# RWKV attention with a gated convolution network: half-row transposes in three sets, receptances and keys by 64-step parts

## The chip, the cores and the metric

The kernel runs on one core of a Trainium2 chip. The metric is the device time of one execution in microseconds (us). A profiled execution gives the trace from which all rows here are taken; its engines are called PE (TensorE, the matrix engine, with PEld for its weight loads), DVE (VectorE), ACT (ScalarE), POOL (GpSimd) and SP (SyncE, which issues nearly all transfers).

## The reference

Inputs are r, k, v, w of shape (4, 8, 768, 48) (batch, heads, steps, head size), u of shape (8, 48), and the weights of a network after it: w_in (384 x 1024), conv_w (3 x 1024), w_out (1024 x 384). The result is (4, 768, 384).

```python
for t in range(S):
    cur = einsum('bhd,bhe->bhde', u[None] * k_t, v_t)
    y[:, :, t] = einsum('bhd,bhde->bhe', r_t, state + cur)
    state = w_t[:, :, :, None] * state + einsum('bhd,bhe->bhde', k_t, v_t)
x = y.transpose(0, 2, 1, 3).reshape(B, S, H * D)
h = maximum(x @ w_in, 0.0)
conv_out = sum over j of conv_w[j] * (h shifted by j - 1 steps, zeros at the ends)
return (h * sigmoid(conv_out)) @ w_out
```

## The kernel before, in words

The 4 x 768 steps are 24 chunks of 128 steps, six to a batch. For each chunk w, k and r are loaded with steps on partitions (tiles `nat`), and TensorE turns them, so that channels lie on partitions and steps along the row: three thirds of 128 channels for each, in a bank of PSUM (`stage_t`, `st["turned"]`: banks wp for decays, kp for keys, rp for receptances). VectorE makes two scans of the decays from wp (L646 backwards, L654 forwards) into the two planes of the tile kr, and multiplies the keys onto plane 0 (L651) and the receptances onto plane 1 (L658). 16-row copies by DMA (L675, "spread") bring the last channels of each head into a fourth third. `stage_b` makes the scores of a chunk on TensorE (L756 for chunks below 8, L764, by halves, from 8 on), puts them under a mask into pm (L796), brings the state forward (L813 or `half_state`, L878), for which the keys are turned back to steps on partitions (bank tb, `turned_back`), and makes the output y of the chunk (L848), which ScalarE and VectorE write as two parts into x (L856, L857).

The network works on eight blocks of 384 steps (`block`). Each of 8 columns of w_in takes three groups of three products (L896), then a chain between ScalarE and VectorE (L908 to L918, `gating`), whose last reader of the bank is the gate L915; three output tiles of a block take eight groups of three products each (L925). A block begins when the x of its chunks and of its neighbours is there, so the first block needs chunks 0 to 3. The weights are brought into two parts of a narrower form first (`convert`, L489 to L497 and L477, L478).

For chunk 8 and later ones (MERGED) the transposes are cut into halves of 64 rows, and two halves that go to different banks run side by side in the two halves of the array. `stage_b` of chunk n issues them for chunk n + 1, together with the way back of chunk n's keys, as two operations of 12 (`f1`, `f2`, function `one_half`). Between the two, VectorE sets the zero columns of wp to zero (`pad`, L598): it waits for `f1`, and `f2` waits for it.

Which operation comes when is not left to a scheduler. `op` only collects operations with what they read and write; `Plan.issue` then issues them in the order of the list ORDER, a number for each operation, and takes the buffer for each new tile from the list PLACES. Every engine works through its own operations in that order. A negative number is a filler product on TensorE (L445), which computes nothing that is used.

Of the kernel before, what the change touches and what calls it, by code (L numbers as in the profile page):

```python
# [25 lines left out]
MERGED = 8  # L26
HALVED = 8
ORDER = [
    1, 3, 2, 49, 174, 173, 5, 7, 6, 8, -8, 11, 19, 14, 180, 53, 10, 13, 50, 15, 18, 20, 16, 51, 9, 177, 0, -8, -8,
    -8, -8, -8, 181, -1, -1, -1, -1, 27, 52, 183, 54, 185, 188, 175, 28, 23, 24, 193, 194, 195, 219, 25, 178, 21,  # L30
    184, 212, 216, 179, 189, 190, 186, 213, 214, 217, 17, 22, 26, 223, -1, -1, -1, -1, 220, -1, -1, -1, 165, 222,
    224, 258, 251, 4, 218, 12, 182, 255, 55, 196, 232, 233, 191, 259, 166, 225, 167, 227, 236, 261, 234, 192, 29,
    221, 203, 168, 170, 228, 169, 58, 204, 205, 253, 252, 200, 235, 197, 201, 171, 187, 71, 198, 65, 257, 229, -2,
    -2, -2, -2, -2, -2, -2, -2, -2, 230, 263, 60, 72, 172, 66, 61, 73, 67, 199, 256, 231, 202, 238, 176, 215, 262,
    56, 59, 237, 57, 267, 242, 206, 208, 209, 245, 264, 266, 268, 269, 207, 271, 272, 74, 68, 239, 69, 244, 243,
    415, 246, 273, 75, 76, 70, 62, 274, 30, 408, 241, 210, 240, 270, 37, 265, 226, 412, 260, 247, 281, 409, 416,
    211, 38, 44, 458, 39, 45, 32, 418, 283, 420, 282, 33, 413, 43, 275, 277, 63, 278, 40, 451, 46, 64, 254, 410,
    453, 452, 77, 419, 248, 421, 423, 279, 280, 286, 287, 276, 455, 31, 249, 414, 41, 288, 284, 250, 436, 424, 289,
    425, 607, 426, 431, 96, 459, 34, 432, 433, 475, 476, 417, 457, 35, 47, 438, 456, 422, -8, -8, 334, 335, 336,
    462, 323, 467, 324, 325, 36, 337, 338, 437, 48, 42, 461, 434, 463, 285, 466, 464, 339, 468, 477, 340, 326, 327,  # L40
    345, 346, 347, 348, 341, 84, 78, 349, 312, 290, 291, 292, 85, 91, 86, 328, 79, 329, 342, 350, 80, 351, 435, 87,
    478, 301, 313, 314, 302, 303, 92, 81, 90, 330, 460, 293, 294, 352, 93, 82, 611, 88, 94, 428, 430, 429, 427, 439,
    83, 89, 95, 109, 315, 441, 110, 614, 295, 331, 111, 296, 411, 445, 446, 442, 472, 474, 469, 470, 473, 471, 454,
    115, 297, 343, 344, 479, 304, 440, 305, 367, 615, 353, 616, 332, 354, 112, 355, 333, 104, 298, 443, 105, 306,
    444, 368, 447, 482, 369, 448, 98, 483, 484, 617, 307, 99, 481, 480, 465, 113, 103, 97, 316, 299, 449, 450, 485,
    486, 487, 308, 488, 356, 357, 358, 522, 523, 500, 489, 490, 524, 501, 502, 106, 114, 100, 609, 300, 107, 613,
    370, 619, 309, 310, 123, 317, 124, 318, 622, 676, 101, 371, 108, 122, 125, 311, 102, 319, 359, 116, 608, 646,
    372, 320, 373, 623, 511, 512, 491, 117, 624, 118, 653, 612, 126, 360, 650, 128, 321, 374, 492, 503, 493, 361,
    375, 362, 618, 620, 513, 654, 656, 631, 119, 120, 363, 364, 376, 655, 648, 647, 134, 674, 675, 365, 514, 135,
    621, 533, 534, 398, 535, 399, 127, 322, 121, 400, 401, 402, 610, 721, 628, 625, 649, 150, 629, 626, 129, 658,  # L50
    130, 661, 136, 494, 137, 142, 366, 131, 377, 536, 651, 525, 515, 141, 526, 132, 495, 496, 138, 652, 139, 133,
    143, 504, 726, 680, 516, 527, 517, 518, 497, 505, 519, 144, 140, 145, 681, 146, 670, 671, 388, 389, 390, 391,
    392, 555, 556, 557, 393, 657, 403, 662, 394, 404, 405, 537, 679, 558, 559, 520, 521, 632, 506, 659, 507, 528,
    635, 637, 529, 538, 663, 539, 508, 560, 530, 561, 395, 636, 540, 541, 406, 396, 566, 567, 568, 685, 641, 686,
    688, 672, 633, 700, 642, 701, 704, 702, 705, 562, 498, 563, 722, 630, 720, 668, 667, 627, 712, 713, 634, 690,
    569, 689, 725, 727, 531, 570, 699, 714, 571, 378, 379, 380, 381, 382, 383, 638, 732, 384, 733, 735, 639, 572,
    749, 640, 750, 753, 751, 754, 385, 544, 545, 546, 669, 769, 665, 771, 664, 666, 678, 710, 770, 532, 761, 673,
    499, 682, 573, 736, 386, 660, 542, 683, 774, 737, 509, 547, 762, 543, 510, 775, 703, 684, 564, 776, 748, 707,
    708, 677, 937, 706, 711, 935, 709, 687, 691, 692, 693, 643, 695, 696, 942, 548, 644, 694, 574, 780, 763, 549,
    697, 550, 698, 781, 551, 940, 645, 552, 587, 588, 589, 783, 740, 577, 760, 757, 758, 759, 724, 756, 755, 723,  # L60
    715, 927, 718, 928, 729, 716, 719, 764, 717, 728, 915, 916, 741, 919, 744, 920, 917, 936, 730, 785, 553, 784,
    742, 914, 743, 731, 941, 777, 766, 779, 565, 767, 768, 765, 578, 579, 580, 734, 782, 788, 581, 590, 591, 738,
    789, 739, 792, 787, 786, 554, 983, 918, 790, 791, 778, 752, 988, 575, 576, 946, 947, 745, 985, 924, 746, 990,
    793, 949, 794, 923, 984, 922, 925, 950, 951, 926, 772, 407, 387, 921, 773, 1191, 975, 592, 593, 594, 747, 795,
    963, 964, 965, 967, 595, 989, 962, 851, 852, 994, 995, 853, 997, 998, 854, 855, 840, 841, 999, 929, 968, 1140,
    1141, 930, 934, 931, 932, 976, 943, 933, 1128, 1129, 1130, 1132, 856, 1133, 857, 796, 842, 843, 844, 845, 797,
    1127, 846, 858, 1146, 1151, 582, 583, 798, 799, 800, 584, 585, 847, 972, 1148, 973, 1147, 1153, 954, 948, 1152,
    1138, 596, 970, 969, 971, 1192, 1193, 939, 974, 1139, 938, 586, 859, 955, 952, 801, 953, 848, 802, 958, 1142,
    807, 808, 809, 818, 860, 810, 957, 811, 819, 820, 1154, 812, 1155, 803, 849, 977, 813, 804, 862, 1157, 1171,
    1172, 1173, 863, 864, 829, 830, 831, 873, 874, 875, 1175, 1158, 821, 956, 944, 865, 822, 814, 1197, 823, 1159,  # L70
    1170, 866, 945, 1176, 815, 850, 1183, 996, 1002, 959, 1240, 1241, 1239, 1179, 1136, 1137, 1134, 987, 1178, 986,
    1135, 1184, 978, 1185, 824, 980, 981, 991, 1231, 979, 861, 1003, 867, 982, 1143, 1145, 1144, 832, 1174, 876,
    833, 1004, 877, 1246, 960, 1245, 1198, 816, 1000, 868, 834, 993, 869, 825, 1005, 992, 1001, 878, 835, 826, 870,
    879, 597, 598, 599, 600, 601, 602, 603, 604, 1006, 1196, 836, 605, 966, 880, 1007, 837, 961, 881, 1202, 1203,
    1008, 1162, 1205, 1163, 1166, 1219, 1156, 1161, 1220, 1223, 1221, 1042, 1064, 1065, 1043, 1044, 1066, 1206,
    1131, 1164, 1207, 1244, 882, 827, 838, 883, 1232, 1279, 1280, 1180, 1177, 1181, 1288, 397, 606, 1454, 1218,
    1165, 1045, 1067, 805, 806, 1046, 1068, 1250, 1160, 1167, 1168, 871, 1224, 1251, 151, 1253, 1267, 1169, 1268,
    1269, 1047, 1271, 1254, 1255, 1075, 1076, 1077, 1020, 1031, 1053, 1054, 1032, 1055, 1021, 1078, 1079, 1266,
    1069, 1048, 1272, 1233, 1080, 1081, 817, 872, 839, 828, 1234, 1186, 1230, 1149, 1182, 1289, 1228, 1187, 1199,
    1188, 1445, 1189, 1190, 1195, 1225, 1287, 1276, 1150, 1229, 1227, 1275, 1194, 1226, 1273, 1503, 1277, 1274, 894,  # L80
    1022, 1009, 1010, 1033, 1011, 1049, 1056, 1057, 1023, 1293, 1270, 1024, 1070, 1071, 1012, 1034, 1035, 1013,
    1201, 1200, 1294, 1281, 1058, 1050, 1082, 895, 896, 1025, 1026, 1059, 1036, 1072, 1014, 1037, 1060, 1083, 1061,
    1015, 1027, 1038, 1016, 1459, 1039, 152, 1028, 1017, 884, 885, 897, 898, 899, 900, 901, 902, 886, 887, 1204,
    1208, 1210, 1258, 1211, 1214, 1212, 1292, 1213, 1247, 1236, 1235, 1209, 888, 889, 1298, 1299, 1259, 1262, 1215,
    1301, 1433, 1249, 1040, 1302, 1248, 1303, 1432, 1260, 1029, 1278, 1453, 1458, 1455, 1501, 1243, 1242, 1238,
    1295, 1237, 1282, 1285, 1284, 1283, 1446, 1286, 1030, 1062, 1493, 1494, 1063, 1252, 890, 891, 904, 905, 906,
    907, 908, 909, 1434, 1435, 1256, 1437, 1438, 1447, 1257, 1300, 1051, 1261, 1216, 1217, 892, 1460, 1084, 1464,
# [234 lines left out]
def rwkv_conv_moe_kernel(  # L322
# [268 lines left out]
    def thirds(t):  # L591
        return t[:, 0:KT * L].rearrange("p (m t) -> p m t", t=L)
# [124 lines left out]
    def stage_b(n):  # L717
# [50 lines left out]
        if MERGED <= after < N:  # L768
# [4 lines left out]
            if "back" in st:  # L773
                reads, wrote = reads + [kr], wrote + [st["back"][3]]
# [16 lines left out]
        if wrote:  # L791
            op("PE", "f2", lambda: one_half(True), [*reads, (nx["turned"][0], 1)], wrote)
            if "back" in st:
                turned_back(n)
# [234 lines left out]
```

## Time and profile before

| What | Value |
|---|---|
| median of 3 runs | 322.68 us (322.6 to 323.31) |
| profiled execution, its own time | 320.73 us |
| span of its trace | 318.6 us |
| PE busy | 310.0 us, 97% of the span |
| DVE busy | 260.9 us, 82% |
| ACT busy | 231.2 us, 73% |
| POOL busy | 207.3 us, 65% |
| first product of the network | 36.28 us after the start |

The span is the time from the first to the last instruction in the trace; the execution's own time is 2.1 us more. Busy times of PE overlap from one matmul to the next, so a duration on PE is no distance; starts are.

### The profile page before, as it was taken

Reading aid. Unit: us, or ns where it says so; the run is one execution under the profiler, and the core shown is the slowest. Engines: PE = TensorE matmul, PEld = TensorE weight load, DVE = VectorE, ACT = ScalarE, POOL = GpSimd, SP = SyncE. Lnnn points to the kernel's source line nnn. Section 1 sums busy time; section 2 is a strip of 40 time slices with the busy share of each in tenths; the row PEclk is TensorE's granted clock in tenths of the full one; section 3 lists DMA queues with packets and bytes.
Section 4 is the critical chain, followed back from the end, with each engine's and each line's share of the span. In section 5 each row is a group of like instructions: output and inputs, shape, how many; then the busy total and the mean of one; then the engine's idle time right before and its main releaser. Section 6 shows DMA issues by size and latency. Waiting matters only on the chain.

```text
span 318.6 us, 11367 instructions
## 1 busy us (share of the span) xinstructions
PE 310.0 (97%) x4470; PEld 288.6 (91%) x4470; DVE 260.9 (82%) x524; ACT 231.2 (73%) x621; POOL 207.3 (65%) x283
## 2 busy tenths in 40 slices
PE   7999999999999999999999899999999999999994
PEld 4888988999898898999998899989999999999994
DVE  4999999999998799989987799868787888555350
ACT  3466889999596588887877688556787887856641
POOL 6768999999898637478289663894083394163320
PEclk9999999999999999999999999999999999999999
DMA  7999368875455457344345555474748300000005
GB/s 154 260 264 231 81 187 223 200 141 175 100 106 111 119 131 160 67 118 87 74 80 125 112 171 128 80 189 89 228 127 277 91 14 2 29 0 1 2 16 187
DMA packets 114079, 39.36 MB, mean 124 GB/s; under 512 B 102605, under 2 KB 109542, under 8 KB 114022
## 3 DMA queue, kind: packets, MB, share of 16 engines
q1 hardware_dynamic: 114020, 38.59, 49.6%
q8 instruction: 36, 0.59, 0.8%
q14 instruction: 21, 0.17, 0.2%
q10 hardware_dynamic: 2, 0.00, 0.0%
HBM read 31.88 MB, written 4.72 MB: 115 GB/s over the span
## 4 chain that ended last, share of the span: by engine, by line
PE 82%; DVE 9%; ACT 3%; issue 2%; POOL 1%; DMA 1%; SPq 1%; DVEq 0%; ACTq 0%
PE bank L925 30%; PE bank L896 27%; PE bank L848 6%; PE bank L780 5%; PE bank L764 3%; PE bank L878 3%; PE bank L756 2%; PE bank L666 2%; PE bank L632 2%; DVE bank L491 1%; DVE kr L646 1%; DVE strip L494 1%; DVE strip L912 1%; PE bank L829 1%; DVE kr L654 1%
## 5 line engine op out<-in xcount | busy, mean ns | idle before, releaser
L896 PE MATMUL bank<-xT,wi 128*128 128x386 f32 x576 | 112.7, 344 | 0.6 <-DVE strip L915 0.5
L925 PE MATMUL bank<-wo,gh 128*128 128x384 f32 x576 | 109.7, 340 | 0.0
L896 PEld LDWEIGHTS bank<-xT,wi 128*128 128x128 f32 x576 | 100.7, 188 | 2.8 <-DVE strip L915 0.8
L925 PEld LDWEIGHTS bank<-wo,gh 128*128 128x128 f32 x576 | 99.6, 188 | 1.3 <-DVE kr L654 0.2
L918 POOL TENSOR_TENSOR gh<-strip,gh 128x384 fp32r<-128x384 f32 x64 | 64.4, 1022 | 53.8 <-ACT gh L917 53.1
L910 DVE SCALAR_TENSOR_TENSOR strip<-bank,cw,strip 128x384 f32<-128x384 f32 x64 | 39.0, 610 | 15.6 <-ACT strip L909 15.2
L914 ACT ACTIVATE strip<-strip 128x384 f32<-128x384 f32 x64 | 32.6, 523 | 17.8 <-DVE strip L912 17.6
L915 DVE TENSOR_TENSOR strip<-bank,strip 128x384 f32<-128x384 f32 x64 | 34.4, 549 | 7.5 <-ACT strip L914 7.0
L684 POOL TENSOR_SCALAR_AFFINE_SELECT pm<-dg 128x1024 f32<-128x1024 f32 x24 | 26.2, 1092 | 21.2 <-PE bank L848 12.2
L912 DVE SCALAR_TENSOR_TENSOR strip<-bank,cw,strip 128x384 f32<-128x384 f32 x64 | 39.0, 612 | 1.1 <-DVE strip L910 0.3
L909 ACT ACTIVATE strip<-bank,cw 128x384 f32<-128x384 f32 x64 | 36.7, 580 | 2.0
L908 ACT ACTIVATE bank<-bank 128x386 f32<-128x386 f32 x64 | 30.1, 477 | 9.8 <-PE bank L896 9.7
L796 DVE COPY_PREDICATED pm<-upper,bank 128x512 f32<-128x512 int32 x48 | 34.1, 736 | 2.4 <-POOL pm L693 0.8
L917 ACT CAST gh<-strip 128x384 fp32r<-128x384 f32 x64 | 31.7, 512 | 5.3 <-DVE strip L915 5.0
L678 POOL TENSOR_TENSOR strip<-nat,nat 128x384 f32<-128x384 f32 x24 | 24.3, 1016 | 6.2 <-DMA nat<-in_k_dram 2.8
L693 POOL COPY pm<-kr 48x256 f32<-48x256 f32 x60 | 23.6, 395 | 6.0 <-DMA kr<-kr 3.0
L680 POOL TENSOR_TENSOR strip<-strip,ubc 128x384 f32<-128x384 f32 x24 | 24.8, 1034 | 2.7 <-issue 1.7
L646 DVE TENSOR_TENSOR_SCAN kr<-bank,one_end 128x387 f32<-128x387 f32 x24 | 23.0, 956 | 3.7 <-PE bank L780 2.6
L848 PE MATMUL bank<-pm,v 128*32 128x64 f32 (+3 forms) x1280 | 25.8, 231 | 0.0
L848 PEld LDWEIGHTS bank<-pm,v 128*32 128x32 f32 (+2 forms) x1280 | 21.8, 109 | 2.0 <-issue 1.2
L654 DVE TENSOR_TENSOR_SCAN kr<-bank,dA 128x387 f32<-128x387 f32 x24 | 23.0, 957 | 0.3
L606 ACT COPY nat<-nat 128x96 f32<-128x96 f32 x72 | 18.6, 268 | 3.5 <-DMA nat<-in_k_dram 1.9
(105 smaller groups left out, 440.6 us busy)
## 6 DMA issues: line engine op xcount, KB each, us to landing
gh<-in_moe_w_out_dram SPq DMA_DIRECT2D x5, 1152.0 KB, 6.6
nat<-in_w_dram SPq DMA_DIRECT2D x24, 192.0 KB, 3.5
nat<-in_r_dram SPq DMA_DIRECT2D x24, 192.0 KB, 3.3
nat<-in_k_dram SPq DMA_DIRECT2D x24, 192.0 KB, 3.9
gh<-in_moe_w_in_dram SPq DMA_DIRECT2D x4, 1152.0 KB
out_dram<-strip SPq DMA_DIRECT2D x24, 192.0 KB, 2.3
v<-in_v_dram SPq DMA_DIRECT2D x32, 96.0 KB, 2.7
kr<-kr SPq DMA_DIRECT2D x120, 16.1 KB, 2.4
```

The lines of the kernel that those rows point to most:

```text
L796: op("DVE", "cp", lambda g=g: nc.vector.copy_predicated(out=pm.t[:, g], mask=upper.unsqueeze(1).to_broadcast([P, NP, L]), data=sc[g].t.rea ...
L848: nc.tensor.matmul(rows(a, 32)[:, ts], lhsT=lhs, rhs=rhs, start=((halved or c == 0) and i == 0), stop=(i == count - 1), skip_group_check=True)
L896: nc.tensor.matmul(t.t[:, 0:xs.stop - xs.start], lhsT=wi[:, m, a, f * P:(f + 1) * P], rhs=xT[:, x0 + m, c, xs], start=(m == 0 and j == 0), ...
L908: ("ACT", "relu", lambda: nc.scalar.activation(out=h(0, width + 2), in_=h(0, width + 2), func=AF.Relu), [t], [t]),
L909: ("ACT", "mul", lambda: nc.scalar.mul(out=a(), in_=h(1), mul=cw[:, 1, fs]), [t, "cw"], [a1]),
L910: ("DVE", "stt", lambda: nc.vector.scalar_tensor_tensor(out=a(), in0=h(0), scalar=cw[:, 0, fs], in1=a(), op0=ALU.mult, op1=ALU.add), [t], ...
L912: ("DVE", "stt", lambda: nc.vector.scalar_tensor_tensor(out=a(), in0=h(2), scalar=cw[:, 2, fs], in1=a(), op0=ALU.mult, op1=ALU.add), [t], ...
L914: ("ACT", "sig", lambda: nc.scalar.activation(out=a(), in_=a(), func=AF.Sigmoid), [], [a1]),
L915: ("DVE", "gate", lambda: nc.vector.tensor_tensor(out=g.t[:, 0:width], in0=h(1), in1=a(), op=ALU.mult), [t, a1], [g]),
L917: ("ACT", "cast", lambda: nc.scalar.copy(out=part(0)[:, 0:width], in_=g.t[:, 0:width]), [g], [key]),
L918: ("POOL", "lo", lambda: nc.gpsimd.tensor_tensor(out=part(1)[:, 0:width], in0=g.t[:, 0:width], in1=part(0)[:, 0:width].bitcast(F32), op=AL ...
L925: nc.tensor.matmul(acc.t[:, 0:DM], lhsT=part(a)[:, tt * P:(tt + 1) * P], rhs=wo[:, f, c, :], start=(f == 0 and a + c == 0), stop=(f == FT ...
```

## The change

From chunk 8 on three sets of half-row transposes take the place of two. The outer sets `f1` (6) and `f2` (6) hold the decays' halves and the keys' way back, the middle one `f1b` (12) the keys and the receptances. The banks kp and rp no longer hold keys and receptances but the first 64 steps of both (`low`) and the last 64 steps of both (`high`). So each of the two products of VectorE makes 64 steps of keys and receptances at once, and both stand behind the second scan; the copy of the first decays into `firsts` stands behind them. The two outer sets and the middle set are collected ahead of the scores; ORDER and PLACES are new lists for all operations of the program, 2175 for 2159, with 34 filler products for 28.

In the new list TensorE's operations around two chunks stand so (in: a group of three products of L896, out: one of L925):

```
before: in x6  f1  in  f2  in x8  hscores/11 hstate/11 hy/10  out x8  hy/11  f1  hstate/12  f2  hscores/12  in x6
after:  in  f1 f1b f2  in x14  hscores/11 hstate/11  out x6  hy/10 hy/11  f1 f1b f2  out  in x3  out  in x2  hstate/12 hscores/12
```

The diff, without the two lists (a new form of each, of the same kind):

```diff
 ORDER = [
...
 PLACES = [
...
@@ -610,6 +611,9 @@
             st["turns"].append((src, lambda m, t=t, pitch=pitch, at=at: t.t[:, m * pitch + at:m * pitch + at + L],
                                 lambda m, src=src: src.t[:, 2 * m:2 * m + 2, :].rearrange("p h d -> p (h d)"), t))
 
+    def by_half(t):
+        return t.t[:, 0:KT * L].rearrange("p (a m t) -> p a m t", a=2, t=HL)
+
     def stage_a(n):
 
         st = chunks[n]
@@ -648,15 +652,26 @@
             op0=ALU.mult, op1=ALU.add), [wp, (wp, 1)], [kr])
         tr(1)
         op("DVE", "small", lambda: nc.vector.reciprocal(out=da.t[:, 0:WID - 1:SL], in_=kr.t[:, 0, 1:WID:SL]), [kr], [da])
-        op("DVE", "kt", lambda: nc.vector.tensor_tensor(out=seg(kr.t[:, 0], 2), in0=thirds(kp.t), in1=seg(kr.t[:, 0], 2),
-                                                        op=ALU.mult), [kp], [kr])
-        op("ACT", "fill", lambda: nc.scalar.copy(out=firsts[:, :, n], in_=kr.t[:, 0, 1:WID:SL]), [kr], [("firsts", n)])
+        if n < MERGED:
+            op("DVE", "kt", lambda: nc.vector.tensor_tensor(
+                out=seg(kr.t[:, 0], 2), in0=thirds(kp.t), in1=seg(kr.t[:, 0], 2), op=ALU.mult), [kp], [kr])
+            op("ACT", "fill", lambda: nc.scalar.copy(out=firsts[:, :, n], in_=kr.t[:, 0, 1:WID:SL]), [kr], [("firsts", n)])
         op("DVE", "scan", lambda: nc.vector.tensor_tensor_scan(
             out=kr.t[:, 1, 0:WID - 1], data0=wp.t[:, 0:WID - 1], data1=da.t[:, 0:WID - 1], initial=0.0,
             op0=ALU.mult, op1=ALU.add), [wp, (wp, 1), da], [(kr, 1)], [kr])
         tr(2)
-        op("DVE", "kt", lambda: nc.vector.tensor_tensor(out=seg(kr.t[:, 1], 0), in0=thirds(rp.t), in1=seg(kr.t[:, 1], 0),
-                                                        op=ALU.mult), [rp], [(kr, 1)], [kr])
+        if n < MERGED:
+            op("DVE", "kt", lambda: nc.vector.tensor_tensor(
+                out=seg(kr.t[:, 1], 0), in0=thirds(rp.t), in1=seg(kr.t[:, 1], 0), op=ALU.mult), [rp], [(kr, 1)], [kr])
+        else:
+            for x, t in enumerate((kp, rp)):
+                def halves_of(x=x):
+                    return kr.t.rearrange("p a w -> p (a w)")[:, 2:2 * WIDE - 2].rearrange(
+                        "p (a w) -> p a w", a=2)[:, :, 0:KT * SL].rearrange(
+                        "p a (m s) -> p a m s", s=SL)[:, :, :, x * HL:x * HL + HL]
+                op("DVE", "kt", lambda t=t, f=halves_of: nc.vector.tensor_tensor(
+                    out=f(), in0=by_half(t), in1=f(), op=ALU.mult), [t], [kr, (kr, 1)])
+            op("ACT", "fill", lambda: nc.scalar.copy(out=firsts[:, :, n], in_=kr.t[:, 0, 1:WID:SL]), [kr], [("firsts", n)])
         if n < EARLY:
             gt = Buf(ps_k)
 
@@ -764,34 +779,33 @@
                         nc.tensor.matmul(sc[g].t[h, m * L + h.start:m * L + h.stop], lhsT=kt(m)[p, h], rhs=rt(m)[p, h],
                                          start=True, stop=True, skip_group_check=True)
         after = n + 1
-        firsts_, seconds, reads, held, wrote = [], [], [], [], []
         if MERGED <= after < N:
             nx = chunks[after]
             wt, kt_, rt_ = nx["turns"]
-            held, wrote = [x[0] for x in nx["turns"]], list(nx["turned"])
-            reads = [t for x in held for t in (x, (x, 1))]
-            if "back" in st:
-                reads, wrote = reads + [kr], wrote + [st["back"][3]]
-            todo = [(rt_, st.get("back")), (wt, kt_)]
-
-            def half(x, g, m):
-                if x is not None:
-                    o, i, p = x[1](m), x[2](m), slice(64 * g, 64 * g + 64)
-                    nc.tensor.transpose(out=o[:, p], in_=i[p], identity=ident[p, p])
-
-            def one_half(second):
-                for a, c_ in (todo if not second else todo[::-1]):
+            back = st["back"]
+            wp, low, high = nx["turned"]
+
+            def half(x, g, m, o):
+                p = slice(64 * g, 64 * g + 64)
+                nc.tensor.transpose(out=o, in_=x[2](m)[p], identity=ident[p, p])
+
+            def outer(first):
+                up, down = (back, wt) if first else (wt, back)
+                for m in range(KT):
+                    half(up, 1, m, up[1](m)[:, HL:L])
+                    half(down, 0, m, down[1](m)[:, 0:HL])
+
+            def inner():
+                for up, down, a in ((kt_, rt_, 0), (rt_, kt_, 1)):
                     for m in range(KT):
-                        lower, upper_ = (a, c_) if not second else (c_, a)
-                        half(upper_, 1, m)
-                        half(lower, 0, m)
-            op("PE", "f1", lambda: one_half(False), reads, wrote)
-            pad(nx["turned"][0], nx["turned"][0:1])
+                        half(up, 1, m, by_half(high)[:, a, m])
+                        half(down, 0, m, by_half(low)[:, 1 - a, m])
+            op("PE", "f1", lambda: outer(True), [wt[0], (wt[0], 1), kr], [wp, back[3]])
+            pad(wp, [wp])
+            op("PE", "f1b", inner, [t for x in (kt_, rt_) for t in (x[0], (x[0], 1))], [low, high])
+            op("PE", "f2", lambda: outer(False), [wt[0], (wt[0], 1), (wp, 1), kr], [wp, back[3]])
+            turned_back(n)
         op("PE", *(("hscores", half_scores) if halved else ("scores", scores)), [kr, (kr, 1), *lasts], sc)
-        if wrote:
-            op("PE", "f2", lambda: one_half(True), [*reads, (nx["turned"][0], 1)], wrote)
-            if "back" in st:
-                turned_back(n)
         for g in range(2):
             op("DVE", "cp", lambda g=g: nc.vector.copy_predicated(
                 out=pm.t[:, g], mask=upper.unsqueeze(1).to_broadcast([P, NP, L]),
```

## Rows read from the trace of the kernel before

**Rows 1.** The page: busy time by engine, and granted TensorE clock in 40 slices.

```profile
PE 310.0 (97%) x4470; PEld 288.6 (91%) x4470; DVE 260.9 (82%) x524; ACT 231.2 (73%) x621; POOL 207.3 (65%) x283
...
PEclk9999999999999999999999999999999999999999
```

**Rows 2.** The page: chain that ended last, share by engine.

```profile
PE 82%; DVE 9%; ACT 3%; issue 2%; POOL 1%; DMA 1%; SPq 1%; DVEq 0%; ACTq 0%
```

**Rows 3.** Groups by line: out<-in, shapes, count, busy us, mean ns, idle before.

```profile
L896 PE MATMUL bank<-xT,wi 128*128 128x386 f32 x576 | 112.7, 344 | 0.6 <-DVE strip L915 0.5
...
L925 PE MATMUL bank<-wo,gh 128*128 128x384 f32 x576 | 109.7, 340 | 0.0
...
L654 DVE TENSOR_TENSOR_SCAN kr<-bank,dA 128x387 f32<-128x387 f32 x24 | 23.0, 957 | 0.3
...
L651 DVE TENSOR_TENSOR kr<-bank,kr 128x384 f32<-128x384 f32 x24 | 13.1, 546 | 0.7
...
L681 DVE TENSOR_REDUCE dg<-strip 128x8 f32<-128x384 f32 x24 | 12.8, 542 | 0.2 <-issue 0.2
...
L650 DVE RECIPROCAL dA<-kr 128x3 f32<-128x3 f32 x24 | 4.1, 170 | 0.3
```

**Rows 4.** PE in order of time, 81 to 119 us: start, duration, line, shapes, count.

```profile
84.79 1.16 PE L756 MATMUL bank<-kr 48*128 48x128 f32 x16
...
85.78 0.22 PE L780 MATMUL bank<-ident,nat 64*128 64x64 f32 x1
...
85.84 0.22 PE L780 MATMUL bank<-ident,nat 64*128 64x64 f32 x1
...
86.97 0.46 PE L780 MATMUL bank<-ident,nat 64*128 64x64 f32 x7
...
87.49 0.79 PE L925 MATMUL bank<-wo,gh 128*128 128x384 f32 x3
...
89.78 1.16 PE L756 MATMUL bank<-kr 48*128 48x128 f32 x16
...
90.88 0.55 PE L813 MATMUL bank<-v,kh 128*32 128x48 f32 x32
...
114.47 0.69 PE L896 MATMUL bank<-xT,wi 128*128 128x386 f32 x3
...
114.99 0.69 PE L925 MATMUL bank<-wo,gh 128*128 128x384 f32 x3
...
115.60 0.68 PE L878 MATMUL bank<-v,kh 64*64 64x48 f32 x32
```

**Rows 5.** DVE in order of time, 0 to 40 us.

```profile
5.57 0.28 DVE L468 TENSOR_SCALAR bank<-strip 24x128 int32<-24x128 int32 x1 [3.50 <-DMA strip<-in_moe_conv_w_dram]
...
35.32 1.00 DVE L857 TENSOR_TENSOR xT<-bank,xT 128x384 fp32r<-128x384 f32 x2
...
36.23 0.55 DVE L658 TENSOR_TENSOR kr<-bank,kr 128x384 f32<-128x384 f32 x1
...
36.69 0.95 DVE L646 TENSOR_TENSOR_SCAN kr<-bank,one_end 128x387 f32<-128x387 f32 x1
...
37.56 0.53 DVE L681 TENSOR_REDUCE dg<-strip 128x8 f32<-128x384 f32 x1
```

**Rows 6.** PE in order of time, 0 to 37 us.

```profile
36.28 0.95 PE L896 MATMUL bank<-xT,wi 128*128 128x386 f32 x4
```

**Rows 7.** PE in order of time, half-row transposes of chunks 8 and 23.

```profile
80.05 0.41 PE L780 MATMUL bank<-ident,nat 64*128 64x64 f32 x7
...
239.67 0.41 PE L780 MATMUL bank<-ident,nat 64*128 64x64 f32 x7
```

**Rows 8.** DVE in order of time, the zero columns of chunks 8 and 23.

```profile
80.81 0.06 DVE L598 MEMSET bank<- 128x4 f32 x1
...
240.16 0.06 DVE L598 MEMSET bank<- 128x4 f32 x1 [0.79 <-PE bank L780]
```

**Rows 9.** PE in order of time, 170 to 178 us.

```profile
176.13 0.27 PE L780 MATMUL bank<-ident,kr 64*128 64x64 f32 x1 [0.85 <-issue]
```

## What the trace leads one to expect

> **What bounds the kernel now.** I read the page first, its busy shares and granted clock [rows 1] and then its chain of work that ended last [rows 2]. TensorE is busy 310.0 of 318.6 us, its clock is at nine tenths or more of full speed in all 40 slices, and 82% of the chain is TensorE's own work. VectorE, the next one, is busy 82%. So from the first product of the gating network to the end, the kernel lasts as long as TensorE's list takes to run through, and a term counts if it shortens that list, puts a hole into it, or moves its beginning.
>
> The groups by line come next [rows 3]: the products with the two weight matrices (L896, L925) take 222 of the 310 us, and the change leaves all 1152 as they are, 384 groups of three. The half-row transposes (L780) are what it rearranges. A "mean ns of one" is no price here, since matmuls overlap; the price is the distance from one start to the next, and TensorE's list in order of time gives it [rows 4]. A group of three big products takes 0.52 us (114.47 to 114.99), but 0.61 when something of another shape follows (114.99 to 115.60). A pair of half-row transposes follows the pair before it after 0.06 us (85.78 to 85.84); a set of twelve takes 0.52 us (86.97 to 87.49), which is six pairs at 0.06 and 0.16 for beginning and end. The sixteen full score products of L756 take 0.99 us when half-row transposes follow them (84.79 to 85.78), and 1.10 when the 32-column state products do (89.78 to 90.88).
>
> Where the list begins is the third thing [rows 5, 6]. The first big product starts at 36.28 us, when VectorE's last piece of x for chunk 3 is made (the second of the two at 35.32). VectorE has work almost without a gap from 5.57 us on, when the conv weights have landed: until then the stretch is VectorE's.
>
> **The change, part by part.**
>
> *Transposes.* The count stays: 24 half-row transposes for each of 16 chunks, in three operations now (6, 12 and 6) where there were two of 12. The price is in the neighbours. Read entry by entry, the old order has 32 separate runs of half-row transposes in TensorE's list from the first big product on, with score, state, output or big products between them; the new one has 23, because the three operations stand side by side for ten chunks and two of them do for five more. Nine runs fewer at 0.16 us [rows 4] are 1.4 us. [...] I counted the places where the shape of the array in use changes (128x128, 64x128, 64x64, 128x32): 104 in the old list, 85 in the new one. The two price rows above give 0.09 to 0.11 us for each (0.61 against 0.52, 1.10 against 0.99). Nineteen times 0.105 are 2.0 us. I take **-2.0**; the bounds are -1.4 (only the runs count) and -3.0 (0.16 for each of the 19).
>
> [...]
>
> *The two products of VectorE.* Before, one product made the keys, between the two scans, and one the receptances. Now each makes 64 steps of both, after the second scan. Elements per product stay at 384 and one input stays in a bank. No row has this form (two planes, three thirds, runs of 64). The nearest are the product itself (L651), 546 ns, and the sum of L681, 542 ns, which reads 384 elements through as many levels [rows 3]. I take 546 as before, cost **0**; were each as slow as a scan (957 ns), 32 products would add 13 us to an engine with 58 us idle, which is in the rivals' hands, not in the sum. What moves is the time at which the keys are ready: a second scan and a product later, 0.87 and 0.46 us by the distances of starts [rows 5], so 1.3 us. Behind the keys wait the 16-row copies by DMA (they waited for the receptances already, so nothing changes for them) and the next chunk's first set, which turns the keys back. In the new list the shortest stretch between a chunk's last transposes and that next set holds eight groups of big products (two of L925, six of L896): 8 x 0.52 and the 0.2 for going to and fro, 4.4 us. The chain beside it is two scans, a reciprocal and two products: 0.87 + 0.17 + 0.87 + 0.46 + 0.55 [rows 3, 5] and, as an estimate, 0.2 us of handing over, 3.1 us. So the cover is there, with 1.3 us to spare: **0**. The copy of the first decays (L653) moves behind the products; only the end reads it.
>
> *The zero column.* VectorE's memset L598 still stands between the two sets that write the decays' bank: it waits for the first, and the second waits for it. Before, another operation stood between, and hid it. Now, for ten chunks, only the middle set does: six pairs at 0.06. From the rows [rows 7, 8]: the twelve transposes of the last chunk end at 240.08 and the memset starts at 240.16, 0.08 later, and takes 0.06. A set of six ends about 0.39 us after its start (0.17 for the third pair, 0.22 for itself), so its memset can end at 0.53, and the last set is due at 0.59. With VectorE free the cover just suffices. But the memset also waits behind what VectorE is doing. At chunk 8 it came 0.35 us after the end of its set (80.46 to 80.81). Over all 16 chunks, of which these are the first and the last, the mean is 0.24 and the longest 0.90; the mean is 0.16 above the least. Ten chunks at 0.16 are 1.6 us; if the new order is placed so that VectorE is free, it is nothing. In the new VectorE list seven of the ten have short or early work ahead of the memset and three have gating steps, so I take **+0.5**, from bounds of 0 and 1.6.
>
> *The head.* Up to the last piece of x of chunk 3 VectorE's list has the same 64 instructions in both orders but for one: eleven scans and eight products now, ten and nine before (a scan of chunk 5, whose first one stood behind, at 36.69, moves ahead). A scan takes the place of a product, 0.87 for 0.46 us by starts [rows 5]: **+0.4**. The lower bound is 0, if the scan falls into a gap. Six more filler products (34 for 28) run while TensorE waits for VectorE; their cover is that wait.
>
> *The rest of the order* moves loads, gating steps and products past each other on all engines. Holes in TensorE's list are the price, and the old one has its own, the longest 0.85 us at 176.13, in the middle of a set and put down to issue [rows 9]. I expect as much of it, **0**; the bounds are -0.85 (that one gone) and +1.7 (two more of its kind).
>
> The sum: -2.0 + 0 + 0.5 + 0.4 = -1.1 us. The profiled execution took 320.73 us (span 318.6); the median of the runs is 322.68, 1.95 above it, and the difference is taken off that: **321.6 us**.
>
> **The rivals.**
> 1. *The memset is late.* Ten chunks wait 0.16 us, as late as VectorE comes to it now: -2.0 + 1.6 + 0.4 = 0, 322.7 us, no change. From 0.15 us on the mean wait eats all that is won. For it speaks VectorE's load of 82%; against it, that at the last chunk, as at most, it stood ready and waiting.
> 2. *Slower: the keys come too late.* The first set of a chunk needs the previous chunk's products, which now stand 1.3 us later in VectorE's list. If VectorE is behind by more than the 1.3 us to spare, TensorE stands still in front of the set. It turns the sign when such waits add up to more than 1.1 us; with two of the full 1.3 us, -1.1 + 2.6 = +1.5, 324.2 us. For it: VectorE takes gating steps of 0.61 us between the links. Against it: most stretches are longer than eight groups.
> [...]
> 4. *More falls away.* The memsets are hidden and the hole goes: -2.0 + 0.4 - 0.85 = -2.5, 320.2 us; with the transposes at their bound of -3.0 it is 319.2.
>
> **How the numbers follow.** Forecast 0.48, rival 1 0.18, rival 2 0.18, rival 3 0.06, rival 4 0.10. A measurement here tells about 0.2%, 0.65 us, from no change. Of the forecast's case (320.8 to 322.4) some 0.08 lies within that; rival 4 is faster, rivals 1 and 3 are no change but for 0.05 that comes out slower, rival 2 is slower. So faster 0.50, same 0.27, slower 0.23. For 8 times in 10 the range reaches into rival 4's span and past rival 2's time: 319.5 to 324.4 us.
>
> **What the profile of the changed kernel would show.** Right: three sets side by side in TensorE's list take about 0.88 us from first start to the next operation; the groups of score products before a set end 0.1 us sooner; the first big product starts near 36.7 us; L598's successor starts 0.06 us after it in a few chunks only. Wrong: a hole in front of the last set that VectorE's memset ends in most chunks (rival 1), one in front of the first set ended by the second product (rival 2), or products of VectorE clearly above 550 ns. The prediction fails most easily by holes that the rearranged order puts elsewhere.

## The result, and the profile after

The changed kernel takes 326.88 us (median of 4 runs, 326.0 to 327.21) against 322.64 us before: a ratio of 1.0125 with a 95% interval of 1.0098 to 1.0152. It is slower, by some 4 us; 321.6 us were predicted, in a range up to 324.4. The profiled execution took 327.12 us, its span is 325.3 us.

The page of the kernel after, busy time by engine and granted clock, which answers to [rows 1]:

```profile
PE 313.3 (96%) x4476; PEld 292.6 (90%) x4476; DVE 263.3 (81%) x524; ACT 229.8 (71%) x621; POOL 206.9 (64%) x283
...
PEclk9999999999999999999999999999997799999999
```

Two slices near 250 us now show the clock at seven tenths. Its chain, which answers to [rows 2], has ACT at 7% for 3% and issue at 3% for 2%:

```profile
PE 79%; ACT 7%; DVE 5%; issue 3%; DMA 2%; POOL 2%; SPq 1%; POOLq 0%; DVEq 0%; ACTq 0%
```

The groups by line, for [rows 3]. The two products of VectorE (L672) cost 553 ns, 7 ns more than L651 did; the idle time of PE in front of L910 is one stop that is put down to issue:

```profile
L910 PE MATMUL bank<-xT,wi 128*128 128x386 f32 x576 | 114.4, 346 | 2.7 <-issue 2.7
...
L659 DVE TENSOR_TENSOR_SCAN kr<-bank,dA 128x387 f32<-128x387 f32 x24 | 23.0, 958 | 0.6
...
L672 DVE TENSOR_TENSOR kr<-bank,kr 128x384 f32<-128x384 f32 x32 | 17.7, 553 | 0.8
```

PE in order of time shows three things. Three sets side by side, where [rows 4] had them apart, take 0.93 us from their first start to the first big product (206.91 to 207.84). The first big product of all starts at 37.02, where [rows 6] had 36.28. And at 246 us, in the middle of a group of L910, TensorE stands still:

```profile
37.02 1.83 PE L910 MATMUL bank<-xT,wi 128*128 128x386 f32 x9
...
206.91 0.27 PE L790 MATMUL bank<-ident,kr 64*128 64x64 f32 x1
...
207.84 1.33 PE L910 MATMUL bank<-xT,wi 128*128 128x386 f32 x6
...
231.94 0.64 PE L790 MATMUL bank<-ident,nat 64*128 64x64 f32 x13 [1.43 <-ACT nat L607]
...
243.00 2.03 PE L862 MATMUL bank<-pm,v 112*32 112x64 f32 x124 [0.31 <-ACT v L900]
...
245.67 0.97 PE L910 MATMUL bank<-xT,wi 128*128 128x386 f32 x4
249.38 2.94 PE L910 MATMUL bank<-xT,wi 128*128 128x386 f32 x8 [2.75 <-issue]
```

The last of these rows is most of the loss. TensorE issues the fourth product of L910 at 246.30 and the next at 249.38, and no engine, semaphore or transfer is named for the wait. Then eight products take 2.94 us; with the full clock twelve take 2.40 (run 4 below). A table by stretches (busy us and count of each engine, granted clock, DMA share, GB/s) shows the clock at 0.66 in the ten microseconds of the stop; the trace's clock record has it at one half for 6.8 us from 248.65 on, so it fell 0.7 us before TensorE went on.

```profile
236.00:246.00 10.00, 9.59 (x304) 8.62 (x303) 6.25 (x14) 8.24 (x23) 8.52 (x15) 1.00 0.65 204
246.00:256.00 10.00, 7.25 (x26) 6.93 (x25) 5.64 (x10) 1.71 (x6) 1.52 (x2) 0.66 0.52 148
256.00:266.00 10.00, 10.00 (x60) 9.96 (x59) 4.61 (x9) 8.03 (x17) 5.25 (x7) 1.00 0.46 155
```

**One account for all runs.** From the first big product on I gave each step in TensorE's list (from one operation's first start to the next one's) the price of an undisturbed step between the same two kinds of operation, the 5% point of all such steps in the traces. The sum of these prices is the floor of a list; what the steps took beyond it is waits. Us:

```
                               first product   floor   waits   of which the longest
before                                 36.28   266.9    11.1   1.1 at 174.8
after                                  37.02   264.1    19.8   3.4 at 246.3, half clock 2.2, 1.6 at 230.1
run 1, old order                       37.50   266.7    18.6   1.7 at 180.2, half clock 1.7, 1.3 at 110.0
run 2, one load later                  36.17   264.1    17.8   1.8 at 275.9, 1.6 at 273.3, 1.6 at 229.9
run 3, order mended                    36.99   264.1    16.9   1.8 at 275.7, 1.6 at 273.1, 1.0 at 244.7
run 4, fewer idle products             36.41   264.1    15.8   1.6 at 231.2
run 5, the changed kernel again        36.82   264.1    21.8   2.9 at 247.8, half clock 1.3, 1.8 at 280.4, 1.6 at 99.3
run 6, more idle products              37.51   264.1    20.4   4.9 at 243.9, half clock 1.5, 1.4 at 230.4
run 7, before, fewer idle products     36.69   266.9    11.0   0.7 at 43.9
run 8, both                            36.45   264.1    16.4   0.9 at 232.5
```

So the change has in fact shortened TensorE's own list, by 2.8 us, and its new order has put 8.7 us of waits into it: 0.7 - 2.8 + 8.7 = 6.6 of the 6.7 us between the two spans. (The profiled execution of before was a quick one, 1.9 us under its median, so the medians are 4.2 us apart.)

The line between floor and waits depends on how finely the steps are told apart, the spans do not. With every pair of operations priced by itself, sets of six and of twelve apart, the two lists differ by 1.6 us (266.2 and 264.6 up to the start of the last big product) and the waits by 7.6; with the follower told apart by its array shape alone, by 2.1 and 8.0. So the list became 1.6 to 2.8 us shorter and the order cost 7.6 to 8.7 us more in waits. The table and what follows keep to 2.8 and 8.7.

### The profile page after: what moved, and what is told of

The parts are those of the page before. It is cut to its first block, busy times and chain, and to the rows that moved or that the text cites. A ratio compares the mean times of both kernels' runs of the same rounds, so it can differ in the third digit from the quotient of the medians.

```text
span 325.3 us, 11368 instructions
## 1 busy us (share of the span) xinstructions
PE 313.3 (96%) x4476; PEld 292.6 (90%) x4476; DVE 263.3 (81%) x524; ACT 229.8 (71%) x621; POOL 206.9 (64%) x283
## 4 chain that ended last, share of the span: by engine, by line
PE 79%; ACT 7%; DVE 5%; issue 3%; DMA 2%; POOL 2%; SPq 1%; POOLq 0%; DVEq 0%; ACTq 0%
PE bank L939 27%; PE bank L910 25%; PE bank L862 7%; PE bank L790 4%; PE bank L771 3%; PE bank L636 3%; PE bank L892 2%; PE bank L681 2%; PE bank L779 2%; PE bank L843 1%; PE bank L446 1%; ACT bank L922 1%; ACT strip L923 1%; DMA nat<-in_k_dram 1%; ACT strip L928 1%
## 5 line engine op out<-in xcount | busy, mean ns | idle before, releaser
L910 PE MATMUL bank<-xT,wi 128*128 128x386 f32 x576 | 114.4, 346 | 2.7 <-issue 2.7
L939 PE MATMUL bank<-wo,gh 128*128 128x384 f32 x576 | 112.0, 343 | 0.0
L910 PEld LDWEIGHTS bank<-xT,wi 128*128 128x128 f32 x576 | 102.4, 191 | 4.3 <-issue 3.5
L939 PEld LDWEIGHTS bank<-wo,gh 128*128 128x128 f32 x576 | 101.0, 190 | 1.2
```

The lines of the kernel that those rows point to most:

```text
L910: nc.tensor.matmul(t.t[:, 0:xs.stop - xs.start], lhsT=wi[:, m, a, f * P:(f + 1) * P], rhs=xT[:, x0 + m, c, xs], start=(m == 0 and j == 0), ...
L939: nc.tensor.matmul(acc.t[:, 0:DM], lhsT=part(a)[:, tt * P:(tt + 1) * P], rhs=wo[:, f, c, :], start=(f == 0 and a + c == 0), stop=(f == FT ...
```

## The experiments

The theory: the stop is TensorE out of code. The trace has 36 packets of 16 KB in a queue of its own, "q8 instruction" (page, part 3), beside another with 21 of 8 KB; the trace has 9102 records on TensorE, 253 for each of the 36. One of these fetches, the 30th, began at 246.93 us, while two loads of weights of 1152 KB each, issued at 238.7 and 240.2 us, were on their way and the DMA engines moved 405 GB/s (in the 2.5 us before). The rival: the instructions of the change, the later keys above all, cost the time in every chunk. Ratios are against the kernel before, run on the same chip; runs 1 to 4 shared one chip, 5 to 8 another.

**Run 1, the change's instructions in the old order.** The code of the changed kernel with the order and the places of before; both products stand behind the second scan (for chunks 11 and 14 ahead of the next `f1`, where the old order had the receptances behind it), `f1b` directly behind `f1`, `f2` where it stood.

```diff
-before: f1 .. f2 ..   scan1 keys scan2 receptances
+run:    f1 f1b .. f2 ..   scan1 scan2 low high
```

> The changed kernel's instructions (three sets of transposes, products of keys and receptances by 64-step halves) in the order of the kernel before: the keys' way back directly behind the decays, the last set where the second set stood, both products behind the second scan. If the order is what cost the time (a code fetch of TensorE held back at 246.9 us, and late fills), this run has no stop near 246 us, the full clock throughout, and 320.5 to 322.8 us: 2.0 us of transposes less, 0 to 2 us given back by keys that come later. If the instructions themselves cost it (the later keys, the zero column between two sets), it loses in every chunk from 8 on and stays at 324.5 to 327 us.

327.51 us, 1.0117 (1.0065 to 1.0169). The waits of PE (us in total, times, longest), and the last of them in order of time:

```profile
PE bank L910 <- DVE kr L672: 2.1, 3, 1.0
PE bank L790 <- DVE kr L672: 1.7, 2, 1.3
PE bank L790 <- issue: 1.4, 1, 1.4
...
181.92 0.27 PE L790 MATMUL bank<-ident,kr 64*128 64x64 f32 x1 [1.45 <-issue]
```

My theory, as I had put it for this run, fell: no stop near 246, but slower all the same. In the old order the keys do come too late, 3.8 us in five places, two in front of a set and three in front of big products whose bank the late products still read; and another stop for issue, at 180.2, is followed by a half clock. (It is a late fetch too, the 21st: it comes after record 5569 of TensorE, as the stop of before at 174.8 [rows 9] does, and run 6 will show what these numbers mean.) And the floor is 266.7, as before: three sets of transposes save nothing while the third stands alone. What the change saves it saves by its order, and without it the late keys are not covered.

**Run 2, one load later.** Of the two loads the second is issued some 20 us later, and its range test (a pass of VectorE and one of ScalarE over the loaded weights) stands behind the next one's.

```diff
-SP: load of w_in 238.7, out, load of w_out 240.2, ...
+SP: load of w_in, out, ..., last out of block 4, load of w_out
```

> The changed kernel with one 1152 KB load of weights (the second of the two that are issued at 238.7 and 240.2 us) issued some 20 us later, its range test behind the next one's. If the code fetch at 246.93 us was late because it stood behind the two loads, it starts by 244.5 us, the stop of 2.75 us at line 910 goes, and with it the stretch at half clock (6.8 us long, about 2.4 us lost): 5.5 us less in the profiled run, 320.7 to 322.5 us timed. If the clock falls for a reason of its own, only the stop goes: 323.3 to 324.5 us. If the stop has nothing to do with the loads, it stays at 326 to 327.2 us.

325.33 us, 1.0039 (1.0009 to 1.0069). The stop is gone, as is the half clock (the row that took its place, of PE in time):

```profile
246.53 1.68 PE L910 MATMUL bank<-xT,wi 128*128 128x386 f32 x8 [0.15 <-issue]
```

The 30th fetch began at 244.22. But the time stays 3 us above what I expected, since the delayed test made its own trouble: two of ScalarE's passes now stand one behind the other, 1.26 us each, and behind them the state copies that the output products of chunk 22 wait for; and a later fetch, the 33rd, is now the late one.

```profile
268.55 1.26 ACT L514 ACTIVATE gh<-gh 128x1152 f32<-128x1152 int32 x1
...
275.01 1.99 PE L862 MATMUL bank<-pm,v 112*32 112x64 f32 x124 [1.36 <-ACT v L760]
278.63 1.22 PE L910 MATMUL bank<-xT,wi 128*128 128x386 f32 x6 [1.62 <-issue]
```

**Run 3, the order mended.** Run 2 and five entries of the lists of ScalarE and SyncE moved ahead by a few places.

```diff
+ACT: both remaining fills of chunk 22 together; keys' copy of chunk 4 first;
+     state copies of chunk 20 ahead of those of 21; a fill ahead of a range test
+SP:  second load of values of chunk 9 ahead of one copy of keys
```

> The changed kernel with the load moved as in the run before it and five entries of ScalarE's and SyncE's order moved ahead by a few places (the third fill of chunk 22, the keys' copy of chunk 4, the four state copies of chunk 20 ahead of those of chunk 21, the second load of values of chunk 9, a fill ahead of a range test). By the sum of the stops in TensorE's list: 5.5 us for the load, 1.4 for the fill, 0.5 for the keys' copy, 0.5 for the state copies and 0.3 for the values, some of it given back by the next wait: 318.0 to 320.5 us. If the losses lie in the instructions and not in the order, 324 us or more.

324.29 us, 0.9999 (0.9967 to 1.0031): 0.4% better than run 2 where I had expected 0.7%. The fill is in time, and the zero column is what ends last there (PE bank L790 <- DVE bank L599, 0.7 us); the earlier keys' copy at 46 us uncovered another wait, 0.61 us for 0.62. The two stops at 273 and 276 us of run 2 are still there, 1.37 and 1.61 us, and one of 1.0 us in the account has come back at 245 us, although the 30th fetch began at 243.85.

The time misses the forecast of 318.0 to 320.5 us and falls under the second case, 324 us or more, by which the losses would lie in the instructions. The profile does not bear that case out: two of the three stops are waits for code, one is for a state copy behind the range tests, and run 4, with the same instructions but for the fillers, has none of the three above 0.5 us. The bound was also set beside 322.64 us; on this chip the kernel before takes 323.76.

**Run 4, fewer idle products.** Nothing is changed but the filler products ahead of the first big product (30 in the first 18 us, four at 36 to 37 us): each pair becomes one of twice the columns.

```diff
-nc.tensor.matmul(bank[:, 0:2 * P], lhsT=warm[:, 0:P], rhs=warm, ...)
+nc.tensor.matmul(bank[:, 0:4 * P], lhsT=warm[:, 0:P], rhs=warm.unsqueeze(1).to_broadcast([P, 2, 2 * P]), ...)
 34 fillers in ORDER -> 18
```

> The changed kernel with the 34 idle products of the first 20 us (256 columns each, results unread) made into 18 of 512 columns: about 32 instructions fewer in TensorE's code for about the same busy time, nothing else touched. If TensorE stopped at 246.4 us because it ran out of code that had been fetched, the piece of code that it has now reaches some 32 instructions further, into big products that take about 0.12 us for each instruction and cover 2.75 us and more: the stop shrinks below 0.5 us, the clock stays up, 320.7 to 322.8 us timed. If the two loads stop TensorE in another way (or a wait that the records don't show does), the stop stays at 2.5 to 3 us and the time at 326 to 327.2 us.

323.51 us, 0.9978 (0.9944 to 1.0012); in us that is above the forecast, which was set beside 322.64 for 323.76 here. No stop, full clock; PE in order of time at the place of the stop, and the stretch that had 0.66:

```profile
246.73 2.40 PE L910 MATMUL bank<-xT,wi 128*128 128x386 f32 x12
...
246.00:256.00 10.00, 10.00 (x75) 9.79 (x72) 9.51 (x17) 5.73 (x13) 1.70 (x3) 1.00 0.57 171
```

An edit more than 200 us ahead of the stop takes it away, with loads, order and data as they were. The fetch itself is as late as ever (table below): it began at 247.91, but 16 products and their weight loads fewer stood ahead, so that the code at hand lasted until 250.19. (The expectation's 0.12 us an instruction is too much: a big product and its weight load, two records, take 0.17 us, so 32 records last 2.8 us.)

**Run 5, the changed kernel again.**

> The changed kernel as it is, beside the kernels that follow and on their chip. If the stop of 2.75 us at 246 us is a fixed property of where the code fetch and the two loads fall, it is there again, 2.3 to 3.4 us long, and the time stands 3.5 to 5 us above the kernel before. If it was a chance of one execution, this profile has none and the time is within 2 us of the kernel before.

328.82 us, 1.0162 (1.0124 to 1.0201). The stop is there again, 2.62 us, and a second of the kind 33 us later (1.65 us, 1.79 in the account). It is no chance of one execution. PE in order of time, and its waits for issue in total:

```profile
250.75 2.02 PE L910 MATMUL bank<-xT,wi 128*128 128x386 f32 x8 [2.62 <-issue]
...
PE bank L910 <- issue: 4.3, 2, 2.6
```

**Run 6, more idle products.** Each filler becomes two of half the columns, 68 for 34. (Line numbers are one higher.)

> The changed kernel with its 34 idle products made into 68 of half the length: some 68 instructions more in TensorE's code ahead of everything, the same columns. If a stop begins where the fetched code ends, it begins 68 instructions earlier, in the short products ahead of line 910 (about 245 us, at the products of chunk 21 or the transposes of chunk 22), ends 2.4 to 2.6 us after the fetch begins, and lasts 2.5 to 4.5 us; 326 to 329 us timed. If the fetch comes earlier by as much as the code is used up earlier, ahead of the two loads' data, the stop is gone instead and the time is 322 to 324 us. If the stop belongs to line 910 and the loads, it stays there at 2.5 to 3 us.

328.78 us, 1.0152 (1.0125 to 1.0179). The stop has left line 910 and stands among the output products, 12 products before their end:

```profile
243.04 1.80 PE L863 MATMUL bank<-pm,v 112*32 112x64 f32 x112 [0.30 <-ACT v L901]
249.28 0.64 PE L863 MATMUL bank<-pm,v 128*32 128x64 f32 x12 [4.44 <-issue]
```

That is the first of my three cases. Counted in TensorE's records in the trace, the stop comes after the same record in all three kernels that have it, though run 6 has 68 more ahead of it (us from the start):

```
                 record 7617   30th fetch   record 7873   the record
                 issued        begins       issued        after it
before           241.46        244.73       247.08        247.26
after            243.28        246.93       246.30        249.38
run 1            248.74        251.29       255.86        256.03
run 2            242.98        244.22       246.04        246.53
run 3            242.27        243.85       245.17        246.26
run 4            244.51        247.91       250.19        250.31
run 5            244.73        248.34       247.79        250.75
run 6            240.77        246.94       244.63        249.28
run 7            241.99        245.31       249.58        249.76
run 8            244.93        248.56       250.55        250.97
```

In no kernel does TensorE go past record 7873 earlier than 2.3 us after the fetch began, and where it was ready sooner it goes on 2.3 to 2.5 us after it. In the kernel before and in run 4 it comes there just as the code does and waits under 0.2 us, in run 8 it waits 0.4. The stops at 276 to 283 us in runs 2, 3 and 5 all come after record 8641, which is 768, three times 256, further on; those of before and run 1 at 175 and 180 us after record 5569, nine times 256 ahead. Counted on in this way, 311 pieces of the ten profiles can be set beside their fetches, and none is used earlier than 2.2 us after its fetch began. So the packets are TensorE's code, and the stop is the wait for one of them. Where the loads stand as in the changed kernel (after, runs 4, 5 and 8) the fetch begins 3.4 to 3.7 us after record 7617, and 6.2 in run 6, where it begins within 0.02 us of its time in after. With the second load moved (runs 2 and 3) it begins 1.2 and 1.6 us after; the median of the 311 is 1.0. So that load held this fetch back, by some 2 us.

Loads are not the only cause of a late fetch, though. The 21st of before came 3.5 us after its record with only 95 GB/s moving; why, no run shows. And a fetch need not be late: the 33rd of run 5 came 1.4 us after its record, and the stop was 1.65 us long, since the short products there used up a piece in 2.4 us.

**Run 7, the control.** The kernel before with 16 idle products of double length for its 28.

> The control: the kernel before with its 28 idle products made into 16 of double length, 24 instructions fewer in TensorE's code. The kernel before has no long stop with a late code fetch but the one of 0.9 us at 176 us; so if only the place of the code matters, the ratio is 0.995 to 1.003. If the longer idle products were themselves what gained in the changed kernel (a shorter or better clocked head), this one gains as much, 1.3 to 1.5 per cent: 0.985 to 0.988.

322.21 us, 0.996 (0.9934 to 0.9985). The longer idle products are not what gained 1.4 to 1.8% in the changed kernel (run 4's 0.9978 against the 1.0125 of the result and the 1.0162 of run 5); here they give 0.4%, and the stop at 174.8 us of before [rows 9] is gone from the profile.

**Run 8, both.** Run 4 with two entries moved ahead: the third fill of chunk 22, and the second load of values of chunk 9.

> The changed kernel with the 18 longer idle products and two entries moved ahead in the order: the third fill of chunk 22 directly behind the first on ScalarE, the second load of values of chunk 9 ahead of one transfer of keys on SyncE. By the stops that stood in the traces it gains 0.8 us (1.60 at 230 us less the 0.84 that the zero column then leaves) and 0.3 to 0.7 us on the run with the longer idle products alone: 1.0 us below that run, some 1.2 to 2.0 us below the kernel before. If the stops are only handed on to the next wait, it equals the run with the longer idle products (ratio 0.998).

322.24 us, 0.9936 (0.9916 to 0.9957). It beats the kernel before by 0.6% and the changed one by more than 2% (1.0162 on this chip). Against run 7, the kernel before with its code moved in the same way, it stands at 0.9936 / 0.996 = 0.998, and the intervals overlap: no difference can be told. Nor can it against run 4 (0.996; the forecast was 0.997). Of the 1.6 us at the fill, 0.87 are left, in front of the zero column.

## Why the prediction was wrong, step by step

*Transposes: size right.* Forecast -2.0 from bounds of -1.4 and -3.0; the floor falls by 1.6 to 2.8. The 0.105 us for a change of shape was an estimate from two pairs of rows [rows 4]; no run varies one such change alone. What the runs show is that cutting two operations into three cost nothing by itself (a floor of 266.7 in run 1 against 266.9 before) and that the gain came with the new neighbours (264.1 with the new order).

*The products of VectorE: right.* 553 for 546 ns. In the new order they make TensorE's weight loads wait 0.5 us in all (0.3 and 0.2, once each), so the cover held; in the old order they cost 3.8. Rival 2 had the right mechanism and was held off by the order.

*The zero column: right.* +0.5 was forecast; the weight loads of L790 wait 0.7 us for L599, in all chunks together. Rival 1 did not come.

```profile
L790 PEld LDWEIGHTS bank<-ident,nat 64*128 64x128 f32 x288 | 14.4, 138 | 2.9 <-ACT nat L607 1.6 <-DVE bank L599 0.7 <-ACT strip L967 0.3
```

*The head: not to be told.* +0.74 in the two profiles for a forecast of +0.4; but with the same head the first big product begins at 36.17, 36.82, 36.99 and 37.02 us in four executions (runs 2, 5, 3 and after).

*"The rest of the order", 0 with bounds of -0.85 and +1.7: the step that failed.* It took the holes of the old list as the price of the new one, without a reason for each, and it measured +8.7 us (+7.6 by the finest prices). Of that the stop is 3.4, the half clock 2.2 (five groups of three big products at 0.44 us more than the full clock's 0.52), and one fill on ScalarE 1.6: the third fill of chunk 22 stands in its list behind an x copy, a gating step and a state copy, and ends at 231.9 for a set that began at 230.1. The rest, 1.5 or less, is a net sum of many places of 0.2 to 0.6 us. With the stop gone (run 4 beside run 7, the same edit in both) the waits are still 4.8 us more than before, against 2.8 us of floor won, in one profile each; the timed ratios differ by 0.2%, within their intervals. So the order gave back what the transposes saved, and the stop made the loss.

Two errors lie in that step. I took the one stop for issue in the old trace [rows 9] as a size for all of them, without asking what it was. It was another late fetch: the 21st began at 173.63, 2.5 us before TensorE went on. What set the size of the stops here was how late the fetch was and where the boundary of a piece fell, and the trace of before had that: its 30th fetch began 3.3 us after record 7617, for 3.6 in after, and cost under 0.2 us for 2.75, as TensorE was in big products by then. And 6 more fillers in the head, which I costed at nothing because TensorE waits there, shift every later boundary by 12 records.

What stays open is the clock. It halved in or within 1.2 us after the stops of 2.75, 2.62, 4.44 and 1.45 us (after and runs 5, 6 and 1), and not at those of 1.36 and 1.62 us of run 2, 1.37 and 1.61 of run 3 or 1.65 of run 5. The shortest stop with it is shorter than the longest without, so the length alone does not tell which; no run here varies the stop alone.

## What to carry to other kernels

Read the stops that the profile puts down to issue against the instruction queue's packets: this program's short products used up a piece in 2.4 us at the 33rd fetch of run 5, and no piece of the 311 was used earlier than 2.2 us after its fetch began; an edit of nothing but idle instructions took the stop away (run 4) or moved it to another place (run 6). Fetches beside large transfers began late here: the eight with over 380 GB/s moving in the 2.5 us before all began more than 3 us after the record where the median of the 311 begins after 1.0. So compare an order with a fixed place of the code in mind, or try each candidate at two or three placements, before believing a difference of 1%. And a long range test or a load that is moved out of the way needs a place on the engine that runs it, not only in the queue that issues it.

## What the runs showed of the hardware

TensorE's code came in pieces of 16 KB (36 packets in before and in after; page, part 3); the stops' places, records 5569, 7873 and 8641, are nine and three times 256 apart, in keeping with 256 to a piece. A fetch took about 1.0 us in its queue (median 0.99 in before, 1.01 in after), and where the engine stood it went on 2.3 to 2.5 us after the fetch began, 2.7 at the 33rd of runs 2, 3 and 5, whose packet took 1.2 to 1.3 us, and 3.4 in run 1, whose packet took 1.85. In after 124 output products of 64 columns ran in 2.0 us, so with their weight loads 256 records lasted about as long as a fetch; at two records in 0.17 us big products would use 256 up in some 22 us, an estimate.

One late piece cost 2.6 to 4.4 us in after and runs 5 and 6, others 0.9 to 1.7 us, and the half clock up to 2.2 us more.

The stop of 2.75 us in after did not come alone: from 0.7 us before its end the granted clock was one half of full speed for 6.8 us, and a group of three big products took 0.96 us instead of 0.52, 2.2 us in the account. Whether the stop brought it on, no run shows.
